# Masked copies of the second half's self probabilities on GpSimd in two operations, with new planned times

## The chip, the cores and the metric

One core of a Trainium2 chip runs the whole kernel. The core has five engines with their own instruction queues: TensorE (PE, with its weight loads as PEld), VectorE (DVE), ScalarE (ACT), GpSimd (POOL) and SyncE (SP), which only issues DMAs. The metric is the device time of one execution in microseconds, as the median of several runs.

## The reference, cut to what matters

The model is one layer: a pre-normalised attention with a recurrent memory, and an MLP. There are 2048 tokens of width 512, 32 heads of width 128, and 64 segments of 32 tokens. Each segment is attended together with 8 memory rows, and the 8 memory rows of the result are the memory of the next segment:

```python
for s in range(n_seg):                                  # 64 segments, in order
    xs = x[:, s * seg_len:(s + 1) * seg_len, :]
    h = jnp.concatenate([mem, xs], axis=1)              # 8 + 32 rows
    q, k, v = (jnp.einsum('btd,dhe->bhte', h, W) for W in (Wq, Wk, Wv))
    scores = jnp.where(mask, jnp.einsum('bhqe,bhke->bhqk', q, k) * scale, -1e9)
    o = jnp.einsum('bhqk,bhke->bhqe', softmax(scores), v)
    o = jnp.einsum('bhte,hed->btd', o, Wo)
    mem = o[:, :M, :]                                   # goes into the next segment
    outs.append(o[:, M:, :])
h = x + concatenate(outs); out = h + mlp(layernorm(h))
```

Because of `mem` the segments can't be computed side by side.

## The kernel before, in words

After a start (segment 0, which also loads the weights), the kernel runs segments 1 to 63, and then the MLP. All four segments of a 128-token block differ a little, since each carries another share of the next block's work.

In each segment, TensorE works through an order written out by hand (`ORDERS`, lines 37 to 40, one for each of the four segments of a block): the projections Q, K and V in two halves of 16 heads each, the score products of the first and the second half (SC0, SC1), units of extra projections for the next block (F0, F1), the probability products (PV0, PV1), the second softmax's product for the segment before (PVA), the output projection (WO) and the second softmax's scores (SA). The rows of a segment are dealt with in two softmaxes. The first, whose chain the change touches, covers the rows that the next segment waits for (`sc_softmax`, lines 1043 to 1065). The second (`sa_mm` and `sa_tail`, tiles SA, nma, sma, rsa, PA, PTA, BD) covers the others and is read a segment later by PVA.

For each half r (0 and 1), `sc_softmax` takes the maximum of the scores on VectorE (line 1045, `nmc`). Two exponentials on ScalarE follow, one for each of two groups sl of columns, each with its sum (line 1054, `EC` and `smc`). VectorE then makes the two reciprocals (line 1059, `rsc`) and two masked copies (line 1062, `PC`). A masked copy multiplies 64 values by the reciprocal and by a mask `even`, which is 1 or 0 by partition, and writes the result twice, once with each column of the mask. Last, VectorE transposes `PC` in blocks of 32 into `PTC` (line 1064). PV0 and PV1 (`pv_c`, line 1075) read `PTC`. The keys of these writes are PCa (sl = 0) and PC (sl = 1), with a 0 or 1 behind them for the half: PCa1 is the masked copy of sl = 0 in the second half. The reciprocals are ra and rsc, the exponentials Ea and EC.

What follows PV0 and PV1 are copies of the result to SBUF (OTm0, OTm1 for the rows that the next segment waits for, OTB for block rows, OTx0 and OTx1 for the rows of PVA), then WO, which reads them, a transpose `TT` (line 1183) and sums into `hT` (line 1177, key hTm), the next segment's memory rows.

The order on the other engines comes from a planner in the kernel (`Sched.schedule`, lines 236 to 344). TensorE's order is fixed, and everything else is taken from a heap as soon as the operations that it depends on are taken. The heap's order is a planned time: `PLAN` (lines 43 to 99) gives for each kind of operation a time from the segment's start, one for each of the four segments of a block. Once taken, an operation goes to the first gap on its engine after its inputs are ready, by estimated durations. So a planned time is a priority, and an operation planned earlier than its inputs is taken right after them. Some operations have several engines to choose from (`S.either`); the cheapest place wins, or the engine named in `HOME`.

Operations marked with `S.narrow` get a dependency on the GpSimd operation ahead of them and give one to that behind them (lines 426 to 428), so that they run strictly one after the other. The four BD copies (line 1132) and the folds of block rows (lines 1217 to 1228) are such. The folds also wait, through `tail` (line 1446), for the second half's last PC and PCa.

Of the kernel before, what the change touches and what calls it, by code (L numbers as in the profile page):

```python
# [26 lines left out]
KEEP = True  # L27
WINDOWS, WIN_LO, WIN_HI = True, 1.0, -0.8
PAUSES, PAUSE_IN, PAUSE_US = 3, 64, 0.5
HALVES = ("kq", "KA", "QT", "ZCm", "VS", "nmc", "Ea", "EC", "ra", "rsc", "PCa", "PC", "PTC", "OTm", "OTx", "KB", "QTB", "VSB")  # L30
BONUS = {}
LEAN = 0.2

# [11 lines left out]
        "ZCm0": (2.85,) * 4,  # L45
        "kq0": (2.23,) * 4,
        "KA0": (2.87,) * 4,
        "SP0": (-1.81, -1.81, -1.52, -1.65),
        "nmc0": (3.86,) * 4,
        "Ea0": (4.18,) * 4,  # L50
        "EC0": (4.59,) * 4,
        "ra0": (4.66,) * 4,
        "PCa0": (4.86,) * 4,
        "rsc0": (5.1,) * 4,
        "PC0": (5.4,) * 4,
        "PTC0": (5.74,) * 4,
        "VS0": (4.88,) * 4,
        "kq3": (2.79,) * 4,
        "QT1": (3.48,) * 4,
        "ZCm1": (3.97,) * 4,  # L60
        "kq1": (3.65,) * 4,
        "KA1": (4.29,) * 4,
        "SP1": (-1.64, -1.64, -1.36, -1.49),
        "nmc1": (5.19,) * 4,
        "Ea1": (5.51,) * 4,
        "EC1": (5.92,) * 4,
        "ra1": (5.98,) * 4,
        "PCa1": (6.1,) * 4,
        "rsc1": (6.35,) * 4,
        "PC1": (6.55,) * 4,  # L70
        "PTC1": (7.13,) * 4,
        "VS1": (6.72,) * 4,
        "OTm0": (6.56,) * 4,
        "OTm1": (7.93,) * 4,
        "OTB": (8.2, 8.48, 8.24, 8.2),
        "SAp": (7.37,) * 4,
        "nma": (10.17,) * 4,
        "SAs": (10.6,) * 4,
        "SAe": (11.07,) * 4,
        "sma": (11.54,) * 4,  # L80
        "rsa": (12.0,) * 4,
        "PA": (12.24,) * 4,
        "PTA": (13.52,) * 4,
        "BD": (15.41,) * 4,
        "OTx0": (7.22, 7.22, 7.71, 7.22),
        "OTx1": (7.71, 8.1, 8.1, 7.71),
        "TT": (9.37,) * 4,
        "hTm": (9.86,) * 4,
        "opA": (17.5, 10.96, 18.73, 17.5),
        "ZCb": (5.92, 3.35, 3.35, 3.35),  # L90
        "kq4": (10.48, 10.48, None, None),
        "KB0": (11.12, None, None, None),
        "QTB0": (None, 28.73, None, None),
        "VSB0": (None, None, 10.48, None),
        "kq5": (9.58, 8.1, None, None),
        "KB1": (12.13, None, None, None),
        "QTB1": (None, 8.75, None, None),
        "VSB1": (None, None, 7.22, None),
        "TTB": (None, None, None, 10.96)}
HOME = {('SC0', 0): 'act', 'ZCm0': 'pool', 'kq1': 'act', 'SP1': 'act', 'VS1': 'act', 'OTm0': 'act', 'SAp': 'dve', 'PA': 'pool', 'VSB1': 'act'}  # L100
STEP = 10.28
# [18 lines left out]
class Op:  # L120
# [3 lines left out]
    def __init__(self, eng, fn, reads, writes, name, dur, mode):  # L124
# [11 lines left out]
        k = writes[0] if writes else ""  # L136
        self.kind = k if isinstance(k, str) else k[0] + (str(k[-1]) if k[0] in HALVES else "")

# [418 lines left out]
ALU = mybir.AluOpType  # L557
# [53 lines left out]
def t_dve(n):  # L611
    return 0.155 + 1.0e-3 * n
# [10 lines left out]
def build_kernel(nc, A_x, A_mem0, A_Wq, A_Wk, A_Wv, A_Wo, B_w1, B_b1, B_w2, B_b2, out):  # L623
    scale = float(E) ** -0.5
    S = Sched(nc)
    st = contextlib.ExitStack()
    with st:
        def sb(name, shape, dt=BF16):
            return st.enter_context(nc.sbuf_tensor(name, shape, dt))
# [45 lines left out]
        OTB = sb("OTB", [P, 2, H, 32])  # L675
# [25 lines left out]
        def sc_place(bank):  # L701

            w = quad[:, bank, 0:128] if bank < 4 else ps[bank][:, 0:128]
            return w.rearrange("p (a n) -> p a n", a=2), ("ps", bank)
# [31 lines left out]
        for sl in range(2):  # L736
            for i in range(4):
# [20 lines left out]
             reads=["maskA"], writes=["maskA"])  # L758
# [200 lines left out]
        def v_B(bk, r, bank, back=False):  # L959
# [6 lines left out]
             reads=["ident"], writes=[("OTB", 1, sg) for sg in range(4)], dur=0.5)  # L966
# [76 lines left out]
        def sc_softmax(s, r, bank):  # L1043
            o, bkey = sc_place(bank)
            S.op("dve", lambda e: e.tensor_reduce(nmc[:, r, :], o, AX.X, ALU.max, negate=True), reads=[bkey], writes=[("nmc", r)], dur=0.28)  # L1045

            b = even[:]
            ev = bass.AP(b.tensor, b.offset, [list(b.ap[0]), [1, 2], [0, 64]])
            last = None
            for sl, names in enumerate((("Ea", "sa", "ra", "PCa"), ("EC", "smc", "rsc", "PC"))):  # L1050
                ek, sk, rk, pk = [(n, r) for n in names]

                def ex(e, sl=sl):
                    return e.activation(EC[:, r, sl, :], o[:, sl, :], ACTF.Exp, bias=nmc[:, r, sl:sl + 1], accum_out=smc[:, r, sl:sl + 1])  # L1054
                x = S.op("act", ex, reads=[("nmc", r)] + [bkey] * sl, writes=[ek, sk], dur=0.37)
                x.prev, last = last, x
            for sl, names in enumerate((("Ea", "sa", "ra", "PCa"), ("EC", "smc", "rsc", "PC"))):
                ek, sk, rk, pk = [(n, r) for n in names]
                S.op("dve", lambda e, sl=sl: e.reciprocal(rsc[:, r, sl:sl + 1], smc[:, r, sl:sl + 1]), reads=[sk], writes=[rk], dur=0.16)
                x = EC[:, r, sl, :]  # L1060
                xc = bass.AP(x.tensor, x.offset, [list(x.ap[0]), [0, 2], [1, 64]])
                S.op("dve", lambda e, sl=sl, xc=xc: e.scalar_tensor_tensor(PC[:, r, :, :, sl], xc, rsc[:, r, sl:sl + 1], ev, ALU.mult, ALU.mult),  # L1062
                     reads=[ek, rk, "even"], writes=[pk], dur=0.305)
            S.op("dve", lambda e: e.transpose(PTC[:, r].rearrange("p k t a -> p (k t a)").bitcast(F32), PC[:, r].rearrange("p k t a -> p (k t a)").bitcast(F32)),
                 reads=[("PCa", r), ("PC", r)], writes=[("PTC", r)], dur=0.31)

        def pv_c(s, r):
            par, bk, sg = s % 2, s // 4, s % 4
# [321 lines left out]
        for s in range(NS):  # L1390
# [66 lines left out]
            def part(name):  # L1457
# [18 lines left out]
                elif name in ("SC0", "SC1"):  # L1476
# [3 lines left out]
                    else:  # L1480
                        prefill("maskCF", maskCF[:].rearrange("p (a t) -> p a t", a=2), 128, o_, k_)
                    sc_mm(s, r, bank_of[name])
                    sc_softmax(s, r, bank_of[name])
                elif name in ("PV0", "PV1"):
                    pv_c(s, r)
# [65 lines left out]
            for n, lo, hi in order:  # L1551
# [4 lines left out]
                elif sg == 3 and n in ("F0", "F1"):  # L1556
                    k = 4 * (n == "F1")
# [55 lines left out]
        for k in range(NSB):  # L1613
# [13 lines left out]
            for t in range(TBS):  # L1627
                for fc in range(FC - lag, FC):
# [3 lines left out]
                     reads=[("ps", t), ("hb", bf, t)], writes=[("ob", bf, t)], after=used["WV"], dur=t_dve(512))  # L1632
# [57 lines left out]
```

## Time and profile before

| | before |
|---|---|
| median of three runs | 809.24 us (807.87 to 809.34) |
| span of the profiled execution | 805.9 us |
| instructions | 43594 |
| PE busy | 775.0 us, 96% |
| VectorE busy | 621.0 us, 77% |
| ScalarE busy | 527.1 us, 65% |
| GpSimd busy | 349.6 us, 43% |

The span goes from the first to the last instruction of the profiled execution. The page gives no other time for that execution; the runs' times hold what lies around the span too, and their median is 3.3 us longer than it. A busy share is an average over the start (to about 52 us), the body of segments 1 to 63 (to about 701 us) and the MLP (the rest). A matmul's row holds its pipelined end, so rows of successive matmuls overlap, and the distance between their starts tells more than their durations.

### The profile page before, as it was taken

How to read it: one execution, taken by the hardware profiler on the slowest of the kernel's cores; microseconds unless marked ns; L12 is line 12 of the kernel's file. 1: busy time of each engine (PE TensorE's matmuls, PEld its weight loads, DVE VectorE, ACT ScalarE, POOL GpSimd, SP SyncE). 2: the span in 40 equal slices, each digit the busy share in tenths (PEclk: the TensorE clock that was granted, in tenths of full speed). 3: DMA queues.
4: the chain of work that ended last, by engine and by line, in shares of the span. 5: the costliest groups of instructions: out<-in, count | busy, mean ns of one | idle time of the engine just before them, and what ended most of it. 6: DMA issues, size and time to landing. Idle time of an engine off the chain costs nothing.

```text
span 805.9 us, 43594 instructions
## 1 busy us (share of the span) xinstructions
PE 775.0 (96%) x19308; PEld 422.5 (52%) x18891; DVE 621.0 (77%) x2008; ACT 527.1 (65%) x1522; POOL 349.6 (43%) x886
## 2 busy tenths in 40 slices
PE   3788999999999999999999999999999999999998
PEld 1345555555555555555555555555555555544443
DVE  3268897989898989898989898989899887824211
ACT  2446777777777777777777777777676766643342
POOL 5023334545454545454545454545463535267200
PEclk9989999999999999999999999999999999999999
DMA  9950010111101010101010202020212131264200
GB/s 340 392 185 16 4 29 11 30 31 29 31 21 39 17 43 17 43 11 50 9 45 10 50 11 50 11 49 3 51 29 62 40 86 29 88 170 130 69 27 26
DMA packets 65449, 48.03 MB, mean 60 GB/s; under 512 B 29028, under 2 KB 61676, under 8 KB 65260
## 3 DMA queue, kind: packets, MB, share of 16 engines
q1 hardware_dynamic: 64928, 44.98, 19.0%
q8 instruction: 150, 2.46, 1.2%
q14 instruction: 39, 0.32, 0.1%
q10 hardware_dynamic: 332, 0.27, 0.1%
HBM read 31.08 MB, written 8.13 MB: 49 GB/s over the span
## 4 chain that ended last, share of the span: by engine, by line
PE 91%; DVE 3%; DMA 2%; SPq 2%; ACT 1%; issue 1%; POOL 0%
PE ps L872 43%; PE ps L1171 16%; PE ps L605 6%; PE quad L1579 6%; PE ps L1572 5%; PE ps L1210 4%; PE quad L1075 3%; DMA WQ<-in_A_Wq_dram 2%; SPq L775 2%; PE ps L1105 2%; PE quad L1037 2%; PE ps L1365 2%; PE quad L1143 1%; PE quad L1080 1%; DVE PC L1062 1%; ACT kq L890 1%
## 5 line engine op out<-in xcount | busy, mean ns | idle before, releaser
L872 PE MATMUL ps<-WQ,hT 128*32 128x512 bf16 x2048 | 157.4, 382 | 3.4 <-DVE hT L1177 3.3
L1171 PE MATMUL ps<-WO,OT 128*32 128x256 bf16 x4224 | 140.8, 275 | 1.0 <-ACT OT L890 1.0
L872 PE MATMUL ps<-WV,hT 128*32 128x512 bf16 x1780 | 138.7, 379 | 0.0
L891 ACT ACTIVATE kq<-ps 128x512 bf16<-128x512 f32 x146 | 87.2, 597 | 63.7 <-PE ps L872 63.4
L1126 POOL TENSOR_TENSOR PA<-SA,rsa 128x256 bf16<-128x256 f32 x64 | 39.9, 624 | 183.0 <-DVE rsa L1119 170.6
L890 ACT CAST kq<-ps 128x512 bf16<-128x512 f32 x160 | 93.4, 584 | 38.2 <-PE ps L872 38.2
L1171 PEld LDWEIGHTS ps<-WO,OT 128*32 128x32 bf16 x4224 | 96.2, 97 | 26.5 <-ACT OT L890 12.3
L1132 POOL COPY BD<-PTA 32x192 bf16<-32x192 bf16 x256 | 95.5, 373 | 16.6 <-DVE PTA L1128 0.8
L1062 DVE SCALAR_TENSOR_TENSOR PC<-EC,rsc,even 128x128 bf16<-128x128 f32 x256 | 94.5, 370 | 6.7
L872 PE MATMUL ps<-WK,hT 128*32 128x512 bf16 x1292 | 92.5, 379 | 0.0
L872 PEld LDWEIGHTS ps<-WQ,hT 128*32 128x32 bf16 x2048 | 57.0, 96 | 57.9 <-issue 18.7
L913 DVE STREAM_TRANSPOSE KALL<-kq 128x256 f32<-128x256 f32 x160 | 70.5, 440 | 20.8 <-ACT kq L890 18.6
L1054 ACT ACTIVATE EC<-quad,nmc 128x64 f32<-128x64 f32 x252 | 77.1, 311 | 5.9 <-DVE nmc L1045 0.2
L605 PE MATMUL ps<-WK,hT 128*32 128x512 bf16 x756 | 74.6, 379 | 0.0
L890 ACT CAST VS<-ps 128x512 bf16<-128x512 f32 x126 | 73.7, 585 | 0.7
L890 ACT CAST OT<-quad 128x128 bf16<-128x128 f32 (+1 forms) x205 | 66.3, 363 | 7.5 <-PE quad L1080 5.7
L913 DVE STREAM_TRANSPOSE QT<-kq 128x256 f32<-128x256 f32 x128 | 57.0, 445 | 15.5 <-ACT kq L891 14.1
L872 PEld LDWEIGHTS ps<-WV,hT 128*32 128x32 bf16 x1780 | 50.5, 96 | 34.2 <-issue 1.0
L1575 ACT ACTIVATE WQ<-ps,b1t 128x512 bf16<-128x512 f32 x42 | 28.9, 688 | 52.0 <-PE ps L1572 52.0
L872 PEld LDWEIGHTS ps<-WK,hT 128*32 128x32 bf16 x1292 | 36.4, 97 | 46.1 <-issue 20.1
L1117 ACT ACTIVATE SA<-SA 128x256 f32<-128x256 f32 x64 | 26.7, 417 | 49.4 <-DVE SA L1116 45.0
L1223 POOL TENSOR_TENSOR opT<-TTB,TTS 32x64 bf16<-32x64 f32 x128 | 40.3, 315 | 31.7 <-DVE opT L1177 22.5
(160 smaller groups left out, 1477.9 us busy)
## 6 DMA issues: line engine op xcount, KB each, us to landing
WV<-in_A_Wv_dram SPq DMA_DIRECT2D x4, 1024.0 KB, 10.3
WK<-in_A_Wk_dram SPq DMA_DIRECT2D x4, 1024.0 KB, 18.0
WQ<-in_A_Wq_dram SPq DMA_DIRECT2D x4, 1024.0 KB, 19.0
WO<-in_A_Wo_dram SPq DMA_DIRECT2D x16, 256.0 KB, 7.6
v_last<-VSB SPq DMA_DIRECT2D x60, 64.0 KB, 3.1
VBD<-v_last SPq DMA_DIRECT2D x60, 64.0 KB, 2.8
h_mid<-xr SPq DMA_DIRECT2D x16, 128.0 KB, 1.8
WQ<-h_mid SPq DMA_DIRECT2D x4, 512.0 KB, 4.4
```

What stands on the lines that cost most here:

```text
L605: return e.add_instruction(mybir.InstMatmult(name="I-%d" % (4000000 + _kept[0]), engine=mybir.EngineType.PE, start_tensor_calc=start, stop ...
L872: ins = e.matmul(o, l, m, start=(k == 0), stop=(k == DC - 1), tile_position=(0, 32 * j), skip_group_check=True)
L890: return {"act": (lambda e: e.copy(out, src), t_act(n, ps_)), "dve": (lambda e: e.tensor_copy(out, src), 0.155 + 1.0e-3 * n * fast)}
L891: return {"act": (lambda e: e.mul(out, src, scale_), t_act(n, ps_)), "dve": (lambda e: e.tensor_scalar(out, src, scale_, None, ALU.mult), ...
L913: S.op("dve", lambda e: e.transpose(out, src), reads=[("kq", i)], writes=[key], dur=t_dve(256) + 0.02)
L1054: return e.activation(EC[:, r, sl, :], o[:, sl, :], ACTF.Exp, bias=nmc[:, r, sl:sl + 1], accum_out=smc[:, r, sl:sl + 1])
L1062: S.op("dve", lambda e, sl=sl, xc=xc: e.scalar_tensor_tensor(PC[:, r, :, :, sl], xc, rsc[:, r, sl:sl + 1], ev, ALU.mult, ALU.mult), reads= ...
L1132: S.narrow(S.op("pool", lambda e, j=j, rows=rows: e.tensor_copy(BD[rows, par, :, j, :, :], PTA[rows, :, 0:NA, :]), reads=["PTA"], writes=[ ...
L1171: ins = e.matmul(ps[bank][32 * j:32 * j + 32, 0:256], lhs(slot(h)), wo_cols(h, b), start=(k == 0), stop=(k == 15), tile_position=(0, 32 * ...
L1223: return e.tensor_tensor(o[32 * q:32 * q + 32, c:c + 2], x, y, ALU.add)
L1572: ins = e.matmul(ps[bank][:, 0:SBT], W1[:, cc, fc * P:(fc + 1) * P], hnT_of(k)[:, cc, :], start=(cc == 0), stop=(cc == DC - 1))
L1579: S.op("pe", lambda e: e.matmul(quad[:, t, :], gT_of(k, fc)[:, t * P:(t + 1) * P], W2[:, fc, :], start=(fc == 0), stop=(fc == FC - 1)), re ...
```

## The change

In segments 1 to 63, for the second half only, the masked copy of sl = 0 leaves VectorE. It was one SCALAR_TENSOR_TENSOR that wrote both copies. It is now two operations on GpSimd, one for each column of the mask, both marked narrow, with the keys PCa1 and PCb1. The transpose into PTC1 waits for both. The first half, and segment 0, stay as they are.

Apart from that, some thirty rows of the planned times are changed, in many cases with another value for each of the four segments. No planned time is given to TensorE, whose order is the same. The rows that belong to the chain above, and the others that are spoken of below:

```diff
-HALVES = (..., "PCa", "PC", "PTC", ...)
+HALVES = (..., "PCa", "PCb", "PC", "PTC", ...)
...
-        "SP0": (-1.81, -1.81, -1.52, -1.65),
+        "SP0": (0.02, 1.04, 0.91, -0.12),
-        "ra0": (4.66,) * 4,
-        "PCa0": (4.86,) * 4,
+        "ra0": (4.39, 4.45, 4.45, 4.39),
+        "PCa0": (1.71, 3.51, 3.81, 3.36),
-        "PTC0": (5.74,) * 4,
+        "PTC0": (4.3, 3.88, 2.35, 3.1),
-        "ra1": (5.98,) * 4,
-        "PCa1": (6.1,) * 4,
-        "rsc1": (6.35,) * 4,
-        "PC1": (6.55,) * 4,
-        "PTC1": (7.13,) * 4,
-        "VS1": (6.72,) * 4,
-        "OTm0": (6.56,) * 4,
-        "OTm1": (7.93,) * 4,
+        "ra1": (5.38, 3.88, 5.23, 6.58),
+        "PCa1": (4.6, 4.75, 5.35, 6.1),
+        "PCb1": (5.89, 4.75, 5.89, 5.89),
+        "rsc1": (6.2, 6.35, 7.25, 4.85),
+        "PC1": (5.29, 6.49, 6.64, 6.49),
+        "PTC1": (5.72, 6.08, 4.88, 5.78),
+        "VS1": (6.03, 5.97, 5.97, 5.97),
+        "OTm0": (5.96, 5.6, 5.9, 5.9),
+        "OTm1": (7.33, 5.98, 7.18, 7.48),
-        "sma": (11.54,) * 4,
+        "sma": (7.88, 7.04, 6.98, 6.68),
-        "BD": (15.41,) * 4,
-        "OTx0": (7.22, 7.22, 7.71, 7.22),
-        "OTx1": (7.71, 8.1, 8.1, 7.71),
+        "BD": (16.07, 16.28, 15.77, 15.47),
+        "OTx0": (6.89, 7.25, 7.29, 6.8),
+        "OTx1": (9.24, 8.13, 9.33, 9.54),
-        "ZCb": (5.92, 3.35, 3.35, 3.35),
+        "ZCb": (2.71, -0.16, -0.16, 0.2),
...
                 x = EC[:, r, sl, :]
                 xc = bass.AP(x.tensor, x.offset, [list(x.ap[0]), [0, 2], [1, 64]])
+                if s > 0 and sl == 0 and r in (1,):
+                    for k in range(2):
+                        S.narrow(S.op("pool", lambda e, k=k, x=x: e.tensor_scalar(PC[:, r, k, :, 0], x, rsc[:, r, 0:1], even[:, k:k + 1], ALU.mult, ALU.mult),
+                                      reads=[ek, rk, "even"], writes=[(("PCa", "PCb")[k], r)], dur=0.25))
+                    continue
                 S.op("dve", lambda e, sl=sl, xc=xc: e.scalar_tensor_tensor(PC[:, r, :, :, sl], xc, rsc[:, r, sl:sl + 1], ev, ALU.mult, ALU.mult),
                      reads=[ek, rk, "even"], writes=[pk], dur=0.305)
             S.op("dve", lambda e: e.transpose(PTC[:, r]..., PC[:, r]...),
-                 reads=[("PCa", r), ("PC", r)], writes=[("PTC", r)], dur=0.31)
+                 reads=[("PCa", r), ("PC", r)] + [("PCb", r)] * (s > 0 and r == 1), writes=[("PTC", r)], dur=0.31)
```

More of the change, by code (lines that the diff above doesn't have):

```diff
@@ L29 @@
 PAUSES, PAUSE_IN, PAUSE_US = 3, 64, 0.5
-HALVES = ("kq", "KA", "QT", "ZCm", "VS", "nmc", "Ea", "EC", "ra", "rsc", "PCa", "PC", "PTC", "OTm", "OTx", "KB", "QTB", "VSB")
+HALVES = ("kq", "KA", "QT", "ZCm", "VS", "nmc", "Ea", "EC", "ra", "rsc", "PCa", "PCb", "PC", "PTC", "OTm", "OTx", "KB", "QTB", "VSB")
 BONUS = {}
@@ L59 @@
         "QT1": (3.48,) * 4,
-        "ZCm1": (3.97,) * 4,
+        "ZCm1": (4.3, 4.36, 4.3, 4.6),
         "kq1": (3.65,) * 4,
         "KA1": (4.29,) * 4,
-        "SP1": (-1.64, -1.64, -1.36, -1.49),
+        "SP1": (-1.58, -2.78, -1.66, -0.23),
         "nmc1": (5.19,) * 4,
@@ L66 @@
         "EC1": (5.92,) * 4,
-        "ra1": (5.98,) * 4,
-        "PCa1": (6.1,) * 4,
-        "rsc1": (6.35,) * 4,
-        "PC1": (6.55,) * 4,
-        "PTC1": (7.13,) * 4,
-        "VS1": (6.72,) * 4,
-        "OTm0": (6.56,) * 4,
-        "OTm1": (7.93,) * 4,
[L75 to L78, printed above, removed]
+        "ra1": (5.38, 3.88, 5.23, 6.58),
[7 more added lines that the diff above has]
+        "OTm1": (7.33, 5.98, 7.18, 7.48),
+        "OTB": (7.72, 9.05, 6.5, 7.6),
+        "SAp": (7.01, 7.22, 6.41, 7.37),
+        "nma": (10.11, 10.56, 10.26, 10.86),
+        "SAs": (10.15, 10.39, 10.15, 10.75),
         "SAe": (11.07,) * 4,
-        "sma": (11.54,) * 4,
-        "rsa": (12.0,) * 4,
-        "PA": (12.24,) * 4,
+        "sma": (7.88, 7.04, 6.98, 6.68),
+        "rsa": (9.6, 11.55, 10.65, 9.15),
+        "PA": (12.09, 11.49, 11.64, 10.89),
         "PTA": (13.52,) * 4,
-        "BD": (15.41,) * 4,
-        "OTx0": (7.22, 7.22, 7.71, 7.22),
-        "OTx1": (7.71, 8.1, 8.1, 7.71),
+        "BD": (16.07, 16.28, 15.77, 15.47),
+        "OTx0": (6.89, 7.25, 7.29, 6.8),
+        "OTx1": (9.24, 8.13, 9.33, 9.54),
         "TT": (9.37,) * 4,
         "hTm": (9.86,) * 4,
-        "opA": (17.5, 10.96, 18.73, 17.5),
-        "ZCb": (5.92, 3.35, 3.35, 3.35),
+        "opA": (17.23, 11.29, 19.66, 18.13),
+        "ZCb": (2.71, -0.16, -0.16, 0.2),
         "kq4": (10.48, 10.48, None, None),
@@ L94 @@
         "VSB0": (None, None, 10.48, None),
[L95 removed]
+        "kq5": (9.64, 8.16, None, None),
         "KB1": (12.13, None, None, None),
         "QTB1": (None, 8.75, None, None),
[L98 removed]
+        "VSB1": (None, None, 6.92, None),
         "TTB": (None, None, None, 10.96)}
```

## The prediction

> **What bounds the kernel now.** I read the page's busy shares first, then the busy time of two stretches of the body, and then the timeline of one segment.
>
> ```profile
> span 805.9 us, 43594 instructions
> PE 775.0 (96%) x19308; PEld 422.5 (52%) x18891; DVE 621.0 (77%) x2008; ACT 527.1 (65%) x1522; POOL 349.6 (43%) x886
> ```
> ```profile
> 92.89:586.90 494.01, 493.97 (x14020) 277.25 (x13404) 443.60 (x1472) 360.86 (x1092) 237.98 (x611) 1.00 0.11 28
> 586.90:691.30 104.40, 102.31 (x2840) 56.84 (x2822) 90.83 (x304) 74.17 (x224) 48.01 (x124) 1.00 0.18 49
> ```
> The columns of the second fence are the length, then PE, PEld, DVE, ACT and POOL busy, then the granted clock. The first row is the 48 segments 5 to 52: 494.01 / 48 = 10.29 us each, with PE never shown idle and the clock full. The second row is the ten segments 53 to 62, 10.44 us each. VectorE is busy 90% of the body, 443.60 / 48 = 9.24 us per segment, and GpSimd 48%. VectorE is the fullest helper, but what counts is where TensorE waits for it.
>
> A segment's timeline (segment 35, from 401.59 to 411.86) shows that, since a busy matmul row includes its pipelined end and so hides short waits. The rows below are TensorE's around the second half (columns: start, duration, engine, line, tiles, count).
>
> ```profile
> 402.47 0.83 PE L872 MATMUL ps<-WQ,hT 128*32 128x512 bf16 x12
> 403.11 0.61 PE L872 MATMUL ps<-WK,hT 128*32 128x512 bf16 x8
> ...
> 407.45 0.40 PE L1210 MATMUL ps<-WO,OTB 128*32 128x512 bf16 x4
> 407.79 0.27 PE L1075 MATMUL quad<-PTC,VS 64*128 64x32 bf16 x8
> ...
> 407.96 0.36 PE L1143 MATMUL quad<-BD,VS 64*128 64x48 bf16 x16
> 408.25 0.40 PE L1210 MATMUL ps<-WO,OTB 128*32 128x512 bf16 x4
> 408.55 0.62 PE L1171 MATMUL ps<-WO,OT 128*32 128x256 bf16 x16
> 409.11 0.27 PE L1075 MATMUL quad<-PTC,VS 64*128 64x32 bf16 x8
> ...
> 409.37 1.50 PE L1171 MATMUL ps<-WO,OT 128*32 128x256 bf16 x48
> 410.69 0.39 PE L1210 MATMUL ps<-WO,OTB 128*32 128x512 bf16 x4
> ```
> Twelve matmuls of 512 columns take 403.11 - 402.47 = 0.64, so a group of four is worth 0.21 us. Forty-eight of 256 columns take 410.69 - 409.37 = 1.32, so sixteen are worth 0.44. From these: the first probability product (PV0, 407.79) comes 0.34 after a group worth 0.21, WO (408.55) comes 0.30 after such a group, and the second product (PV1, 409.11) comes 0.56 after WO's sixteen, worth 0.44. A change of matmul shape takes some 0.1 of the first and the third. So PV0 may lose 0.02, WO 0.09, PV1 about nothing. These small waits are all that the body can win. The rows that end just before:
>
> ```profile
> 406.83 0.29 DVE L1045 TENSOR_REDUCE nmc<-quad 128x2 f32<-128x128 f32 x1
> 407.04 0.35 DVE L1062 SCALAR_TENSOR_TENSOR PC<-EC,rsc,even 128x128 bf16<-128x128 f32 x1
> 407.43 0.31 DVE L1064 STREAM_TRANSPOSE PTC<-PC 128x128 f32<-128x128 f32 x1
> 407.66 0.12 DVE L1059 RECIPROCAL rsc<-smc 128x1 f32<-128x1 f32 x1
> 407.82 0.37 DVE L1062 SCALAR_TENSOR_TENSOR PC<-EC,rsc,even 128x128 bf16<-128x128 f32 x1
> 408.08 0.16 DVE L1059 RECIPROCAL rsc<-smc 128x1 f32<-128x1 f32 x1
> 408.28 0.36 DVE L1062 SCALAR_TENSOR_TENSOR PC<-EC,rsc,even 128x128 bf16<-128x128 f32 x1
> 408.67 0.31 DVE L1064 STREAM_TRANSPOSE PTC<-PC 128x128 f32<-128x128 f32 x1
> ```
> ```profile
> 407.66 0.20 ACT L1054 ACTIVATION_READ_ACCUMULATOR EC<-quad,nmc 128x1 f32 x1
> 407.75 0.58 ACT L890 CAST VS<-ps 128x512 bf16<-128x512 f32 x1
> 408.21 0.67 ACT L890 CAST OT<-quad 128x128 bf16<-128x128 f32 x2
> ```
> The first half's transpose ends at 407.43 + 0.31 = 407.74 and PV0 starts at 407.79: 0.05 from one engine to the other, so PV0 does wait for VectorE. The second half's ends at 408.67 + 0.31 = 408.98; with the same 0.05 PV1 could start at 409.03, and it starts at 409.11. It has 0.08 us to spare. WO stands behind ScalarE's first OT cast, which itself follows the VS cast without a gap.
>
> **The change, part by part.**
>
> Removed: one SCALAR_TENSOR_TENSOR per segment in segments 1 to 63, the one at 407.82. It is 0.37 long, but the next instruction starts 408.08 - 407.82 = 0.26 later, so VectorE gets 63 x 0.26 = 16 us of its queue back. It belongs to the r=1 chain alone, which ends in PV1. The r=0 chain, which PV0 waits for, keeps all its instructions. The max over the second half's scores (key 5.19) still stands ahead of PC0 (5.4), so the new times don't reorder it either: PTC0 is now taken as soon as PC0 is placed, but nothing on VectorE stood between them.
>
> Added: two TENSOR_SCALAR per segment on GpSimd, each 128x64, f32 in, bf16 out. The trace has no such row. The nearest:
>
> ```profile
> L1254 POOL TENSOR_SCALAR rst<-agg 128x1 f32<-128x1 f32 x16 | 3.5, 222 | 15.9 <-DVE agg L1253 14.9
> L1223 POOL TENSOR_TENSOR opT<-TTB,TTS 32x64 bf16<-32x64 f32 x128 | 40.3, 315 | 31.7 <-DVE opT L1177 22.5
> L1225 POOL COPY TTS<-TTB 64x256 f32<-64x256 f32 x32 | 12.6, 393 | 36.2 <-DVE opT L1177 34.4 <-DVE TTB L1214 0.9
> ```
> One element takes 0.22, 64 elements of two inputs 0.315, 256 of one input 0.39. So one costs between 0.22 and 0.39; I take 0.29, near the 64-element row. Both are marked narrow, so that each waits for the one ahead of it, like the BD copies:
>
> ```profile
> 403.38 0.20 DVE L1119 RECIPROCAL rsa<-sma 128x8 f32<-128x8 f32 x1
> 403.66 0.62 POOL L1126 TENSOR_TENSOR PA<-SA,rsa 128x256 bf16<-128x256 f32 x1 [1.51 <-DVE rsa L1119]
> 405.91 1.68 POOL L1132 COPY BD<-PTA 32x192 bf16<-32x192 bf16 x4
> 407.11 0.47 POOL L1132 COPY BD<-PTA 32x192 bf16<-32x192 bf16 x1
> 408.96 0.29 POOL L829 COPY hB<-xT 128x128 bf16<-128x128 bf16 x1 [1.38 <-DMA xT<-xn]
> ```
> From VectorE to GpSimd takes 403.66 - 403.58 = 0.08. The first three BD copies take 407.11 - 405.91 = 1.20, so 0.40 each, of which about 0.06 is the step between narrow ones. GpSimd is free from 405.91 + 1.68 = 407.59 to 408.96. The queue is open, then: the first reciprocal ends at 407.78, PCa1 runs 407.86 to 408.15, PCb1 408.21 to 408.50, and with 0.08 back (taken equal to the way there; no row shows it) PTC1 could start at 408.58 instead of 408.67. Meanwhile VectorE does the second reciprocal as soon as ScalarE's accumulator has been read (407.66 + 0.20 = 407.86), then PC1 at about 408.10 to 408.47. Gain at PTC1: 0.09, and PV1 starts where it does, because it did not wait. With 0.22 each the gain is 0.23 and equally hidden. With 0.39 each PTC1 starts at 408.78, 0.11 late, of which 0.08 is slack: 0.03 lost per segment, 2 us in all.
>
> PC1 and the new pair both read EC, at the same time. The trace shows what that does: the fourth BD copy, issued at 407.11 while the SCALAR_TENSOR_TENSOR of 407.04 runs, takes 0.47, where the three before it keep a step of 0.40. So I count 0.13 us for an operation that comes second (0.47 less the 0.34 that a step of 0.40 leaves). PCb1 then ends at 408.63 and PTC1 starts at 408.71, 0.04 late and inside the slack. Were the second to wait for the whole of the first, PCb1 would start at 408.47 and end at 408.76, and PTC1 would start at 408.84: 0.17 late, 0.09 beyond the slack, 5.6 us over 62 segments. Against that stands the BD row: its 0.47 is less than the 0.28 that the other still had to run and a copy's 0.34 together. The Trainium skill (SBUF — State Buffer, "Who interferes with whom") has the harder rule: a VectorE instruction with two SBUF inputs contends with a GpSimd instruction that reads SBUF, and the later one fully blocks; by it the sum would be 5.6 us up, while the trace agrees with a wait but not with a full one.
>
> Where PV1 does wait, something can be won. In five segments without the extra projections (2, 3, 60, 61 and 62) the row of WO and that of PV1 stand further apart:
>
> ```profile
> 68.73 0.62 PE L1171 MATMUL ps<-WO,OT 128*32 128x256 bf16 x16 [0.16 <-ACT OT L890]
> 69.50 0.25 PE L1075 MATMUL quad<-PTC,VS 64*128 64x32 bf16 x7 [0.16 <-DVE PTC L1064]
> ...
> 676.55 0.27 PE L1075 MATMUL quad<-PTC,VS 64*128 64x32 bf16 x8 [0.38 <-DVE rsc L1059]
> ...
> 687.67 0.62 PE L1171 MATMUL ps<-WO,OT 128*32 128x256 bf16 x16 [0.16 <-ACT OT L890]
> 688.32 0.25 PE L1075 MATMUL quad<-PTC,VS 64*128 64x32 bf16 x7
> ```
> From WO to PV1 it is 0.77 in the first of the five and 0.65 in the last, against 0.56. The gain is 0 to 0.1 in each; I take half: 0.25 us.
>
> Moved: the planned times. They are priorities; an operation is placed in the first gap after its inputs are ready. Most moves ask for a time before its inputs (sma from 11.54 to about 7, PTC0, ZCb), which means "at once". The second softmax has room: BD ends at 407.59 and its reader starts at 407.96, even if BD's key grows by 0.6. The mask copies SP0 and the cast OTx1 go later, into the segment's idle stretches; if they collide with the hT sums at a segment's end, each 0.1 costs 6 us, but the sums' keys did not move. In every fourth segment VectorE is full up to the transpose TT:
>
> ```profile
> 441.72 0.18 DVE L807 BATCH_NORM_AGGREGATE agg<-stt 128x2 f32<-128x6 f32 x1
> 441.82 0.42 DVE L1183 STREAM_TRANSPOSE TT<-ps 128x256 f32<-128x256 f32 x1
> ```
> Here the shorter queue can pull TT forward by up to 0.04, 15 x 0.02 = 0.3 us. No DMA is added or moved past another.
>
> Sum: -0.25 - 0.3 = -0.5 us on a profiled span of 805.9. What lies around the span is 809.24 - 805.9 = 3.3 us and stays; so 808.7 for the median.
>
> **The rivals.**
>
> *The new order frees the first half (faster).* If the re-planned second softmax and casts let PC0 pass the max reduction, PV0 gets back its 0.02 in 57 segments (1.1 us), and in each of the five segments without projections, where it idles for 0.38 (the row of 676.55), the 0.21 by which the max holds PC0 up (406.83 to 407.04): 1.0 us. That is -2.1, 807.1. If WO's 0.09 went too, another 5 us: that is the low end. For it: VectorE's 16 us of room and the many keys that changed. Against it: nmc1, PC0 and rsc0 keep their keys, and ScalarE's two casts stand ahead of WO without a gap.
>
> *GpSimd's pair ends PTC1 late (slower).* It decides from the point where the pair ends after 408.67 + 0.08 - 0.08 = 408.67, that is 0.38 per operation with its waits. Price beyond that: 0.05 late is 62 x 0.05 = 3.1 us, 812.3; a full wait behind PC1 is 814.3, and of the chance below it holds 0.05. For it: two operations that read what VectorE reads. Against it: the 0.315 row has two inputs, the new ones have one.
>
> *The relief is real and not seen.* PV1's slack only grows: 809.2; it shares the forecast's case.
>
> **How the numbers follow.** This kernel's runs lie within 1.5 us, so 0.2% (1.6 us) is about what can be told from no change. Forecast and unseen relief: 0.43. First half freed, wholly or in part: 0.36. GpSimd late: 0.21. The predicted time is the forecast's, 808.7. Its own range is 807.5 to 809.8; with the others' bounds the range is 804.5 to 812.3.
>
> **What would show it.** In the profile after: SCALAR_TENSOR_TENSOR x193 instead of x256, VectorE some 16 to 23 us less busy, 126 new GpSimd rows of 0.22 to 0.39. PTC1 should start within 0.1 of 408.67 - 401.59 = 7.08 after its segment's start, and PV1 0.56 after WO. A PV1 at 0.60 or more after WO is the slow rival, a PV0 gap of 0.32 or less the fast one. A body of other than 10.2 to 10.35 us per segment makes the prediction wrong.

## The result: 2.4% slower, and the profile after

| | before | after |
|---|---|---|
| median of four runs | 808.62 us | 827.48 us (827.33 to 827.73) |
| ratio to before, with its 95% interval | | 1.0239 (1.0226 to 1.0251) |
| span of the profiled execution | 805.9 us | 825.7 us |
| one of the segments 5 to 52 | 10.29 us | 10.64 us |

The forecast was 808.7 us with a range of 804.5 to 812.3. The change cost 19 us instead. The page of after, and the same two stretches of the body (length, then PE, PEld, DVE, ACT and POOL busy, granted clock):

```profile
span 825.7 us, 43784 instructions
PE 784.0 (95%) x19308; PEld 420.0 (51%) x18891; DVE 615.1 (74%) x1961; ACT 523.6 (63%) x1506; POOL 401.8 (49%) x1012
...
L1065 POOL TENSOR_SCALAR PC<-EC,rsc,even 128x64 bf16<-128x64 f32 x126 | 52.2, 414 | 26.0 <-ACT EC L1055 19.7
```
```profile
93.94:604.42 510.48, 502.18 (x14022) 275.02 (x13407) 439.59 (x1437) 358.34 (x1080) 277.39 (x706) 1.00 0.11 27
604.42:710.98 106.56, 102.99 (x2840) 56.76 (x2822) 89.11 (x296) 73.68 (x222) 56.62 (x145) 1.00 0.18 48
```

The 48 segments take 510.48 instead of 494.01 us: 16.5 of the 19.8 us by which the span grew. The last ten give another 2.2 us. The clock is full in both, and TensorE, which before showed no idle time here (493.97 of 494.01), now shows 510.48 - 502.18 = 8.3 us of it. About half of the loss thus shows as idle time; a matmul's row, which holds its pipelined end, can hide the rest. Every kind of segment is longer (the table below). The row of line 1065 is the added work: 126 instructions as foretold, but of 0.414 us each.

The lines of VectorE (count, then busy time and mean ns, then idle time ahead of them and what ended it) show the work removed, x193 where before had x256, and a new wait:

```profile
L1070 DVE STREAM_TRANSPOSE PTC<-PC 128x128 f32<-128x128 f32 x128 | 39.9, 312 | 31.8 <-POOL PC L1065 29.6
L1068 DVE SCALAR_TENSOR_TENSOR PC<-EC,rsc,even 128x128 bf16<-128x128 f32 x193 | 70.9, 368 | 4.4
L1013 DVE COPY ps<-maskAF 128x256 f32<-128x256 f32 x31 | 12.4, 400 | 0.0
```

VectorE now stands idle for 29.6 us ahead of the transposes until GpSimd's last PC is there. The third row is one that the planner moved, the copy of maskAF: it runs on VectorE 31 times, in before twice:

```profile
L1012 DVE COPY ps<-maskAF 128x256 f32<-128x256 f32 x2 | 0.9, 428 | 0.0
```

Segment 35 of after lasts from 412.81 to 423.55. Its timeline on TensorE, then VectorE, then GpSimd (start, duration, engine, line):

```profile
412.81 0.41 PE L873 MATMUL ps<-WQ,hT 128*32 128x512 bf16 x4
...
418.67 0.40 PE L1216 MATMUL ps<-WO,OTB 128*32 128x512 bf16 x4
419.02 0.27 PE L1081 MATMUL quad<-PTC,VS 64*128 64x32 bf16 x8
...
419.77 0.62 PE L1177 MATMUL ps<-WO,OT 128*32 128x256 bf16 x16
420.52 0.27 PE L1081 MATMUL quad<-PTC,VS 64*128 64x32 bf16 x8
...
420.78 1.50 PE L1177 MATMUL ps<-WO,OT 128*32 128x256 bf16 x48
...
423.55 0.41 PE L873 MATMUL ps<-WQ,hT 128*32 128x512 bf16 x4 [0.17 <-DVE hT L1183]
```
```profile
419.31 0.37 DVE L1068 SCALAR_TENSOR_TENSOR PC<-EC,rsc,even 128x128 bf16<-128x128 f32 x1
420.15 0.31 DVE L1070 STREAM_TRANSPOSE PTC<-PC 128x128 f32<-128x128 f32 x1 [0.48 <-POOL PC L1065]
420.39 0.40 DVE L1013 COPY ps<-maskAF 128x256 f32<-128x256 f32 x1
420.82 0.52 DVE L1183 TENSOR_TENSOR opT<-TT 64x96 bf16<-64x96 f32 x2
421.35 0.56 DVE L891 CAST OT<-quad 128x384 bf16<-128x384 f32 x1
421.83 0.41 DVE L1250 TENSOR_TENSOR xr<-xr,oN 128x512 bf16<-128x512 bf16 x1
422.28 0.43 DVE L1255 BATCH_NORM_STATS2 st<-xr 128x6 f32<-128x256 bf16 x1
422.62 0.43 DVE L1189 STREAM_TRANSPOSE TT<-ps 128x256 f32<-128x256 f32 x1
```
```profile
419.11 0.94 POOL L1065 TENSOR_SCALAR PC<-EC,rsc,even 128x64 bf16<-128x64 f32 x2 [0.30 <-ACT EC L1055]
```

PV0 follows its WO group after 419.02 - 418.67 = 0.35 (before 0.34), so the first half is as it was. PV1 follows WO after 420.52 - 419.77 = 0.75 (before 0.56): 0.19 late. The rows say why: GpSimd's pair ends at 419.11 + 0.94 = 420.05, PTC1 starts at 420.15, and VectorE, done with PC1 at 419.68, waits. The other rows show a second loss: everything on VectorE behind PTC1 has moved with it. The last rows of this queue in segment 35 of before (from 401.59), behind PTC1 at 408.67, and one of ScalarE's:

```profile
408.91 0.52 DVE L890 CAST OT<-quad 128x384 bf16<-128x384 f32 x1
409.46 0.62 DVE L1177 TENSOR_TENSOR opT<-TT 64x96 bf16<-64x96 f32 x2
410.09 0.43 DVE L1244 TENSOR_TENSOR xr<-xr,oN 128x512 bf16<-128x512 bf16 x1
410.55 0.43 DVE L1249 BATCH_NORM_STATS2 st<-xr 128x6 f32<-128x256 bf16 x1
410.91 0.45 DVE L1183 STREAM_TRANSPOSE TT<-ps 128x256 f32<-128x256 f32 x1
```
```profile
408.74 0.42 ACT L1012 COPY ps<-maskAF 128x256 f32<-128x256 f32 x1
```

TT, the transpose that hT and so the next segment waits for, started 410.91 - 401.59 = 9.32 after the segment's start. In after it starts at 422.62 - 412.81 = 9.81, right behind BATCH_NORM_STATS2. That is 0.49 late, where PV1 is 0.19 late; the segment is 0.47 longer (10.74 for 10.27). PTC1 is 0.26 late here (7.34 for 7.08). The other 0.23 is a longer queue: from PTC1 to TT it is 410.91 - 408.67 = 2.24 in before and 422.62 - 420.15 = 2.47 in after. The same instructions stand between the two, the cast in another place, and ahead of them the copy of maskAF, which ScalarE did in before.

The same from the traces of all versions, over the twelve segments of each of the four kinds in a block (segments 5 to 52; kind 3 is the one shown). PV1 behind WO is a median, the length a mean, both worked out from the trace. By its medians WO starts 6.96 to 6.99 after the segment's start in every version:

```
               PV1 behind WO          segment length, by kind 0 to 3      mean
before         0.55 0.55 0.55 0.55    10.30 10.33 10.28 10.27             10.29
after          0.74 0.75 0.74 0.74    10.55 10.58 10.70 10.70             10.64
split_only     0.74 0.74 0.74 0.74    10.46 10.57 10.76 10.48             10.57
plan_only      0.55 0.55 0.55 0.57    10.30 10.33 10.27 10.43             10.33
one_on_pool    0.55 0.55 0.55 0.55    10.29 10.29 10.43 10.41             10.36
pair_const     0.55 0.55 0.55 0.55    10.30 10.32 10.44 10.50             10.39
told           0.68 0.68 0.68 0.67    10.41 10.50 10.42 10.38             10.43
told_swapped   0.75 0.75 0.75 0.74    10.49 10.57 10.52 10.45             10.51
wait_order     0.67 0.67 0.68 0.67    10.49 10.51 10.63 10.66             10.57
one_tt         0.62 0.62 0.62 0.62    10.34 10.44 10.58 10.57             10.48
one_tt_newplan 0.62 0.62 0.62 0.55    10.39 10.45 10.58 10.44             10.46
```

PV1 is equally late in all four kinds of after, but the segments are 0.25 to 0.44 longer. Where the second loss falls depends on the planned times: in split_only, which has those of before, it is largest in kind 2.

### The profile page after: what moved, and what is told of

It is laid out like the page before. It is cut to its first block, busy times and chain, and to the rows that moved or that the text cites. A ratio compares the mean times of both kernels' runs of the same rounds, so it can differ in the third digit from the quotient of the medians.

```text
span 825.7 us, 43784 instructions
## 1 busy us (share of the span) xinstructions
PE 784.0 (95%) x19308; PEld 420.0 (51%) x18891; DVE 615.1 (74%) x1961; ACT 523.6 (63%) x1506; POOL 401.8 (49%) x1012
## 5 line engine op out<-in xcount | busy, mean ns | idle before, releaser
L1177 PE MATMUL ps<-WO,OT 128*32 128x256 bf16 x4224 | 143.7, 275 | 1.7 <-ACT OT L891 1.0
L1068 DVE SCALAR_TENSOR_TENSOR PC<-EC,rsc,even 128x128 bf16<-128x128 f32 x193 | 70.9, 368 | 4.4
L891 ACT CAST OT<-quad 128x128 bf16<-128x128 f32 (+1 forms) x191 | 61.0, 350 | 19.1 <-PE quad L1086 17.6
L1065 POOL TENSOR_SCALAR PC<-EC,rsc,even 128x64 bf16<-128x64 f32 x126 | 52.2, 414 | 26.0 <-ACT EC L1055 19.7
L1070 DVE STREAM_TRANSPOSE PTC<-PC 128x128 f32<-128x128 f32 x128 | 39.9, 312 | 31.8 <-POOL PC L1065 29.6
```

The source lines that it names most:

```text
L891: return {"act": (lambda e: e.copy(out, src), t_act(n, ps_)), "dve": (lambda e: e.tensor_copy(out, src), 0.155 + 1.0e-3 * n * fast)}
L1065: S.narrow(S.op("pool", lambda e, k=k, x=x: e.tensor_scalar(PC[:, r, k, :, 0], x, rsc[:, r, 0:1], even[:, k:k + 1], ALU.mult, ALU.mult), r ...
L1177: ins = e.matmul(ps[bank][32 * j:32 * j + 32, 0:256], lhs(slot(h)), wo_cols(h, b), start=(k == 0), stop=(k == 15), tile_position=(0, 32 * ...
```

## The experiments

**The code alone (split_only).** The planned times are those of before, with PCb1 at PCa1's 6.1.

```diff
-        "PCa1": (4.6, 4.75, 5.35, 6.1),
-        "PCb1": (5.89, 4.75, 5.89, 5.89),
+        "PCa1": (6.1,) * 4,
+        "PCb1": (6.1,) * 4,
...
```

> The code part alone: the two GpSimd copies with the planned times of before (PCb1 gets PCa1's 6.1). Theory A (the pair's price): PTC1 starts 0.2 us late in every segment as in the changed kernel, PV1 follows, and the in-order VectorE queue behind PTC1 delays the rest; the planned times add nothing that can be measured: 825 to 830 us. Theory B (the planned times cost the part that PV1's own 0.19 us x 62 = 12 us leaves): 819 to 822 us.

It took 824.59 us, 1.0218 (1.0196 to 1.0239) of before: nearly the whole loss, with PV1 0.74 behind WO as in after. That is 0.4 us below the range of Theory A, and well above Theory B's.

**The planned times alone (plan_only).** The masked copy stays one SCALAR_TENSOR_TENSOR on VectorE.

```diff
-                if s > 0 and sl == 0 and r in (1,):
-                    for k in range(2): ...
-                    continue
```

> The planned times alone: VectorE keeps its SCALAR_TENSOR_TENSOR. Theory A: within 1.6 us of before, 807 to 810.5 us. Theory B: 5 to 8 us slower than before, 814 to 817 us.

809.00 us, 1.0014 (1.0000 to 1.0027): at most a small loss. In the profiled execution it lies in one kind of segment (10.43 instead of 10.27). The new times bring nothing by themselves, and the two parts add up to the whole within their intervals.

**One of the two on GpSimd (one_on_pool).** The first column of the mask stays on GpSimd, the second is a TENSOR_SCALAR on VectorE, with the planned times of before.

```diff
+                    S.narrow(S.op("pool", lambda e, x=x: e.tensor_scalar(PC[:, r, 0, :, 0], x, rsc[:, r, 0:1], even[:, 0:1], ALU.mult, ALU.mult),
+                                  reads=[ek, rk, "even"], writes=[("PCa", r)], dur=0.41))
+                    S.op("dve", lambda e, x=x: e.tensor_scalar(PC[:, r, 1, :, 0], x, rsc[:, r, 0:1], even[:, 1:2], ALU.mult, ALU.mult),
+                         reads=[ek, rk, "even"], writes=[("PCb", r)], dur=0.22)
```

> As split_only, but only the copy with the mask's first column is on GpSimd; the one with the second is a TENSOR_SCALAR on VectorE. GpSimd's single copy would end some 6.72 us into the segment, before PC1 on VectorE. Theory A: PTC1 starts within 0.1 us of where it did before and the loss is gone, 807 to 812 us. If what hurts is that VectorE and GpSimd read EC at the same time, or the hand-over itself, some 5 to 10 us of the loss stay: 814 to 820 us.

810.61 us, 1.0041 (1.0026 to 1.0056). The single operation is 0.448 us, 0.03 more than one of the pair (tile PC by line, min, median and max ns), and PV1 is on time:

```profile
L1064 POOL TENSOR_SCALAR PC<-EC,rsc,even x63: 442/448/456, 57.6 to 700.7; 128x64 bf16<-128x64 f32 x63
```

So it is the second operation in a row on GpSimd that makes PV1 late. The rest, some 3 us, lies in two kinds of segment, of which below.

**What each form costs on an idle chip (price).** Before, with four of each of nine forms on GpSimd, one after the other, on spare tiles in the MLP, where GpSimd and VectorE have little to do.

```diff
+        probe(lambda e: e.tensor_scalar(st_, xs_, r_, ev_, ALU.mult, ALU.mult))    # L1647
+        probe(lambda e: e.tensor_scalar(ct_, xs_, r_, ev_, ALU.mult, ALU.mult))    # L1648, dense output
+        probe(lambda e: e.tensor_scalar(st_, xs_, r_, None, ALU.mult))             # L1649
+        probe(lambda e: e.tensor_scalar(st_, xs_, 0.5, 1.0, ALU.mult, ALU.mult))   # L1650
+        probe(lambda e: e.tensor_scalar(st_, xs_, 0.5, None, ALU.mult))            # L1651
+        probe(lambda e: e.tensor_copy(st_, xs_))                                   # L1652
+        probe(lambda e: e.tensor_tensor(st_, xs_, xs_, ALU.mult))                  # L1653
+        probe(lambda e: e.tensor_scalar(st_[:, 0:1], xs_[:, 0:1], r_, ev_, ALU.mult, ALU.mult))   # L1654
+        probe(lambda e: e.tensor_tensor(PC[:, 1, :, :, 0], xb_, evb_, ALU.mult))   # L1655
```

> The kernel before with nine forms of a GpSimd operation, four of each, on scratch tiles in the last part of the MLP, where GpSimd and VectorE are idle; time as before. If the 0.41 us of a TENSOR_SCALAR is its own price, the same form (128x64, f32 in, bf16 out, two pointer scalars) takes 0.40 to 0.42 here too. If it is contention with VectorE's reads, it takes 0.27 to 0.32. Among the forms, the one without the second scalar, the ones with constants, the one with a dense output and the one with a single element tell which of them carries the price.

It took 808.25 us in its one run. Tile PC by line (min, median and max ns, first and last start), and the first four on the timeline:

```profile
L1647 POOL TENSOR_SCALAR PC<-EC,rsc,even x4: 412/414/416, 782.8 to 784.4; 128x64 bf16<-128x64 f32 x4
L1648 POOL TENSOR_SCALAR PC<-EC,rsc,even x4: 393/394/394, 784.9 to 786.4; 128x64 bf16<-128x64 f32 x4
L1649 POOL TENSOR_SCALAR PC<-EC,rsc x4: 457/463/481, 786.9 to 788.5; 128x64 bf16<-128x64 f32 x4
L1650 POOL TENSOR_SCALAR PC<-EC x4: 262/263/264, 789.1 to 790.1; 128x64 bf16<-128x64 f32 x4
L1651 POOL TENSOR_SCALAR PC<-EC x4: 387/388/390, 790.5 to 791.9; 128x64 bf16<-128x64 f32 x4
L1652 POOL CAST PC<-EC x4: 255/257/259, 792.3 to 793.3; 128x64 bf16<-128x64 f32 x4
L1653 POOL TENSOR_TENSOR PC<-EC x4: 295/295/296, 793.7 to 794.8; 128x64 bf16<-128x64 f32 x4
L1654 POOL TENSOR_SCALAR PC<-EC,rsc,even x4: 337/340/343, 795.2 to 796.5; 128x1 bf16<-128x1 f32 x4
L1655 POOL TENSOR_TENSOR PC<-EC,even x4: 402/402/404, 796.9 to 798.4; 128x128 bf16<-128x128 f32 x4
```
```profile
782.83 1.96 POOL L1647 TENSOR_SCALAR PC<-EC,rsc,even 128x64 bf16<-128x64 f32 x4 [25.15 <-ACT WQ L1577]
```

The form of the change costs 0.414 with nothing beside it, exactly what it costs in after: its price is its own, not contention with PC1. It is not the strided output either (0.394 dense). It is the scalars read from SBUF: two constants in their place cost 0.263, and with pointers even a single element costs 0.340. Four take 1.96 us, so the step from one narrow operation to the next is (1.96 - 4 x 0.414) / 3 = 0.10. The pair therefore needs 0.414 + 0.10 + 0.414 = 0.93 us, as after shows (0.94).

**The pair at the price I had assumed (pair_const).** After, with constants instead of the two scalars. It leaves out the reciprocal and the mask of these copies.

```diff
-e.tensor_scalar(PC[:, r, k, :, 0], x, rsc[:, r, 0:1], even[:, k:k + 1], ALU.mult, ALU.mult)
+e.tensor_scalar(PC[:, r, k, :, 0], x, 0.015625, float(1 - k), ALU.mult, ALU.mult)
```

> The changed kernel with constants in place of the two pointer scalars of the GpSimd pair; what it leaves out is the reciprocal and the mask in that group of columns. Each operation should take 0.26 us instead of 0.41. Theory A (what counts is when the pair ends): the pair ends 6.93 us into the segment instead of 7.23, PTC1 starts at about 7.04, PV1 is on time at about 7.52, and the time is 807 to 811 us. If the hand-over through GpSimd itself costs the time, or the planned times, it stays above 815 us.

812.96 us, 1.0051 (1.0031 to 1.0072), above the expected range by 2 us. PV1 is on time in every segment (0.55). The pair ends 6.97 us into the segment and PTC1 starts at 7.08 (medians), both 0.04 later than expected. The first operation of a pair takes 0.263 us, but the second takes 0.342. It starts while PC1 runs on VectorE (in the segment from 393.85 it starts at 400.49, and PC1 runs from 400.35 to 400.72). Still, that PTC1 lies within 0.1 of the 7.08 that the prediction asked for; what was lost with it is what the price of 0.414 costs, 1.0239 - 1.0051 = 1.9%, 15 us. But about 4 us remain that PV1 has no part in. They lie in kinds 2 and 3. In kind 2, ScalarE's rows and the VectorE cast ahead of them (segment from 393.85):

```profile
401.17 0.98 DVE L891 CAST OT<-quad 128x384 bf16<-128x384 f32 x2
```
```profile
401.72 0.27 ACT L1013 COPY quad<-maskCF 128x128 f32<-128x128 f32 x1 [0.16 <-DVE OT L891]
401.92 0.26 ACT L891 CAST OT<-quad 128x128 bf16<-128x128 f32 x1
```

ScalarE's last cast for WO starts 401.92 - 393.85 = 8.07 after the segment's start, where before it starts at 7.89 (median of this kind). A mask copy has been put ahead of it, and that waits for VectorE's cast. Segments of this kind are 0.16 longer. The trace of one_on_pool, which has the planned times of before, shows the same mask copy ahead of the same cast (8.05) in the same two kinds. In kind 3 of pair_const the cast is early, and it is VectorE's queue up to TT that is late (TT 9.55 instead of 9.33). So these 3 to 4 us are places that the planner chose anew once the operation had left VectorE. I read that off the traces; no run takes it away alone.

**What the planner believes (told).** After, with the pair's estimated duration at 0.5 each instead of 0.25; the same instructions, perhaps in other places.

```diff
-                                      reads=[ek, rk, "even"], writes=[(("PCa", "PCb")[k], r)], dur=0.25))
+                                      reads=[ek, rk, "even"], writes=[(("PCa", "PCb")[k], r)], dur=0.5))
```

> The changed kernel, but the planner is told 0.5 us for each GpSimd operation instead of 0.25, so that it places what follows on VectorE and ScalarE by a true time; the instructions are the same. Theory A1 (PV1's own lateness, 0.19 us x 62 = 11.6 us, stays, and the other 7 us come from a VectorE and a ScalarE queue filled in the belief that the pair is short): 818 to 822 us. Theory A2 (the other 7 us follow from the late PV1 whatever the order): 825 to 829 us.

815.65 us, 1.0091 (1.0073 to 1.0109): 12 us better than after with the same pair, and below what either theory allowed. VectorE in segment 35 (from 404.90), and GpSimd:

```profile
411.40 0.37 DVE L1068 SCALAR_TENSOR_TENSOR PC<-EC,rsc,even 128x128 bf16<-128x128 f32 x1
411.68 0.43 DVE L1013 COPY ps<-maskAF 128x256 f32<-128x256 f32 x1
412.17 0.31 DVE L1070 STREAM_TRANSPOSE PTC<-PC 128x128 f32<-128x128 f32 x1
```
```profile
411.20 0.93 POOL L1065 TENSOR_SCALAR PC<-EC,rsc,even 128x64 bf16<-128x64 f32 x2 [0.30 <-ACT EC L1055]
```

The mask copy that stood behind the wait is now ahead of it, and fills it. It is so in all segments of kinds 0 and 3, where in after the copy stood right behind PTC1. Besides, the pair ends at 411.20 + 0.93 = 412.13 and PTC1 starts 0.04 later, where in after it was 0.10. That I had not expected. The two programs differ at PTC1 in one thing: the transpose waits for two counts, VectorE's own and GpSimd's, and told lists them in the other order. The kernel itself sorts an instruction's waits by their planned end, the latest first (line 462 of after); with 0.25 per operation it plans the pair's end before PC1's, with 0.5 behind it. Two runs change that order alone.

**The order of the two waits (wait_order, told_swapped).** In wait_order, after's PTC1 waits for GpSimd first and then for VectorE's own count. In told_swapped, told's PTC1 waits in the order of after.

```diff
+                    if o.kind == "PTC1":
+                        o.waits = sorted(o.waits, key=lambda p: p.eng != "pool")     # told_swapped: != "dve"
```

> The changed kernel with the same instructions in the same order; only PTC1 waits for GpSimd's semaphore first and for VectorE's own second, instead of the other way round. In the changed kernel PTC1 starts 0.10 us after the pair's end, in the run told, which had this order, 0.035 us. If the order of the two waits makes that difference: PTC1 and PV1 0.07 us earlier in each segment, 62 x 0.07 = 4 us, 822 to 825 us. If it came from the other order of the VectorE queue in told: as the changed kernel, 826 to 829 us.

> The run told, with PTC1's two waits in the order of the changed kernel (VectorE's own first). If the order of the waits is worth 4 us: 818.5 to 821 us, and the rest of the way to the changed kernel's 827 us is what the planner's false price does to the VectorE and ScalarE queues. If it is worth nothing: 814 to 817 us.

wait_order took 823.20 us, 1.0188 (1.0169 to 1.0207); told_swapped 820.53 us, 1.0163 (1.0143 to 1.0182): both lie in the range for an order that counts. In wait_order's segment 35 the last of the pair and the transpose:

```profile
417.59 0.42 POOL L1067 TENSOR_SCALAR PC<-EC,rsc,even 128x64 bf16<-128x64 f32 x1
```
```profile
418.04 0.31 DVE L1072 STREAM_TRANSPOSE PTC<-PC 128x128 f32<-128x128 f32 x1 [0.40 <-POOL PC L1067]
```

418.04 - (417.59 + 0.42) = 0.03, against 0.10 in after. PV1 moves by the same 0.07 in both pairs of runs (0.74 to 0.67, 0.68 to 0.75). With after and told the four make a square, in ratios to before:

| | own count first | GpSimd's first |
|---|---|---|
| planner told 0.25 | 1.0239 (after) | 1.0188 |
| planner told 0.5 | 1.0163 | 1.0091 (told) |

The order of two waits is worth 0.0051 and 0.0072, which is 4 to 6 us of 809 (62 x 0.07 = 4.3). The planner's wrong price, with the order of the waits the same, is worth 0.0076 and 0.0097, 6 to 8 us. Since that price also set the order, all of 1.0239 - 1.0091 = 1.5%, 12 us, comes from it. What remains in told is 0.0091 or 7.4 us, as much as PV1's remaining lateness of 0.12 would cost: 62 x 0.12 = 7.4.

**One GpSimd operation without pointers (one_tt, one_tt_newplan).** VectorE multiplies the mask by the reciprocal (128x2), and one TENSOR_TENSOR of 128x128 on GpSimd writes both copies; in one_tt with the planned times of before, in one_tt_newplan with the new ones.

```diff
+                    S.op("dve", lambda e: e.tensor_scalar(re[:], even[:], rsc[:, r, 0:1], None, ALU.mult), reads=[rk, "even"], writes=[("PCb", r)], dur=0.13)
+                    S.op("pool", lambda e, xc=xc, re_=re_: e.tensor_tensor(PC[:, r, :, :, 0], xc, re_, ALU.mult),
+                         reads=[ek, ("PCb", r)], writes=[("PCa", r)], dur=0.45)
```

> The planned times of before, and one GpSimd operation in place of the pair: VectorE multiplies the two mask columns by the reciprocal (128x2), and GpSimd multiplies EC by that in one TENSOR_TENSOR of 128x128, 0.40 us in the idle part of the MLP. The result is the whole computation. It should end about 6.85 us into the segment and PTC1 start at about 6.98, 0.1 earlier than before. Theory A: 806 to 809 us, at most 0.5 us of gain, since PV1 did not wait before. If any hand-over through GpSimd costs time: 811 us or more.

> As one_tt, with the new planned times. Theory A: as the planned times alone, 807 to 811 us. If the new times are worth something once the GpSimd part ends early, 803 to 806 us.

one_tt took 819.34 us, 1.0131 (1.0115 to 1.0148), one_tt_newplan 817.09 us, 1.0108 (1.0092 to 1.0125). one_tt is 10 us above its Theory A, and one_tt_newplan lies above both of its ranges. GpSimd and VectorE in one of its segments (from 407.84), then the same in one_tt_newplan (from 406.88):

```profile
414.38 0.40 POOL L1067 TENSOR_TENSOR PC<-EC,re 128x128 bf16<-128x128 f32 x1 [0.54 <-DVE rsc L1061]
```
```profile
414.40 0.55 DVE L1070 SCALAR_TENSOR_TENSOR PC<-EC,rsc,even 128x128 bf16<-128x128 f32 x1
415.05 0.31 DVE L1072 STREAM_TRANSPOSE PTC<-PC 128x128 f32<-128x128 f32 x1
```
```profile
413.55 0.44 POOL L1067 TENSOR_TENSOR PC<-EC,re 128x128 bf16<-128x128 f32 x1 [0.67 <-DVE re L1066]
```
```profile
413.37 0.37 DVE L1070 SCALAR_TENSOR_TENSOR PC<-EC,rsc,even 128x128 bf16<-128x128 f32 x1
414.02 0.31 DVE L1072 STREAM_TRANSPOSE PTC<-PC 128x128 f32<-128x128 f32 x1 [0.27 <-POOL PC L1067]
```

The GpSimd operation costs its 0.40 and ends at 414.78, in time. But VectorE's PC1, issued 0.02 behind it, takes 0.55 instead of 0.37 and ends at 414.95; it sets PTC1. PTC1 then starts 0.10 behind PC1's end, where in before, with a single wait, it is 0.03 (so also the medians over segments 5 to 52). Here GpSimd's count is listed first and VectorE's own, the one that comes last, second: the price of the second place again, though the engine is another. Of the 0.12 by which PTC1 is late (7.21 for 7.10), 0.04 is PC1's later end and 0.07 this. Where the order is the other way round, in the second version, PC1 takes 0.37, the GpSimd operation 0.44, and PV1 in that kind of segment is on time (0.55). So here two engines do stand in each other's way, and the one issued first wins. The Trainium skill (SBUF — State Buffer, "Who interferes with whom") states that order of issue decides, for a VectorE instruction with two SBUF inputs beside a GpSimd instruction that reads SBUF; these rows agree with that. They don't agree with a full block, which that section states for a VectorE instruction in a 2-port mode and the prediction counted for this one: PC1 issued at 414.40 and held until 414.78 would end at about 415.15, and it ends at 414.95. Nor is the rule seen in after, where PC1 starts inside the first TENSOR_SCALAR of the pair (419.31, with it running to 419.52) and takes 0.37 as ever.

At 62 x 0.07, PV1's lateness would make 4.3 of one_tt's 10.6 us. The rest lies mainly in kinds 2 and 3, 0.30 longer each. There the same mask copy as in pair_const stands ahead of ScalarE's last cast for WO, which starts at 8.20 instead of 7.89. No run takes that away alone.

No version that was run beats before.

## Why the prediction was wrong

**The mechanism was a rival in it, and its size was wrong.** "GpSimd's pair ends PTC1 late" had a chance of 0.21, with the point of decision at 0.38 per operation and a price of 3.1 us. It is what happened, at six times that price.

The step that failed first is "so one costs between 0.22 and 0.39; I take 0.29". The upper bound was itself below the truth of 0.414. I bounded by the number of elements, and all three rows lacked what sets this price: the scalars read from SBUF. The trace of before held a sign that the number of elements is no bound: a GpSimd TENSOR_TENSOR of one element (line 809, `rst<-rst,cneg`, a power) takes 0.57. The row of 0.222 is a TENSOR_SCALAR of one element without a pointer; with two pointers one element costs 0.340. I had bounded from both sides, but with rows that all lay on one side in this respect, and I did not open the bound for it.

The smaller terms of the same sum: the step between narrow operations was 0.10 and not 0.06, the hand-over from GpSimd to VectorE 0.10 and not 0.08, and the contention of 0.13 did not occur: the second operation takes 0.417, the first 0.412 (medians). The longer first operation had pushed the second nearly past PC1 (419.62, with PC1 done at 419.68). In pair_const, where it starts earlier, the second takes 0.08 more than the first, so the term was not empty. In all the pair with its hand-over took 0.94 + 0.10 = 1.04 where the sum had 408.71 - 407.86 = 0.85 with contention. PTC1 came 7.33 after the segment's start (before 7.10), 0.24 late; PV1 came 0.19 late, so 0.05 of the slack that I put at 0.08 was there.

**Lateness times 62 gives 12 of the 19 us.** The rival's price counted PV1 alone. That fits where the planner knows the price: told loses 7.4 us with PV1 0.12 late, and told_swapped 13 with PV1 0.19 to 0.20 late. But by it after would lose 62 x 0.19 = 12 us, and it lost 19. I had asked what is queued behind SCALAR_TENSOR_TENSOR and not what is queued behind PTC1, which now waits at the head of VectorE's queue for 0.48 us (29.6 us over the kernel). A planner that believes 0.25 per operation puts copies behind the wait instead of ahead of it, and they hold up TT. With the waits in the same order and PV1 equally late, told_swapped is 6 us faster than after.

**Planned times.** The 0.3 us from a shorter queue in every fourth segment did not come: even in pair_const TT of that kind (2) starts later, 9.49 instead of 9.37. Alone, the new times cost at most 0.3%. "VectorE some 16 to 23 us less busy" failed also: it was 621.0 - 615.1 = 5.9 us. The planner filled the room with copies and casts from ScalarE (the maskAF copies grew from 0.9 to 12.4 us). The gain of 0.25 us in the segments without projections is too small to be told from anything here.

**What held:** x193 and x126 as counted, the first half and WO where they were (WO at 6.96 to 6.99 in all versions), the sign of the slow rival (PV1 at 0.60 or more behind WO), and that VectorE's relief is worth nothing while TensorE sets the pace: even with the pair on time, pair_const is not faster.

## What to carry to other kernels

Work that leaves a busy engine for an idle one must be priced by the very form of the instruction, the kind of its scalars included; where the trace has no row with the same operands, the upper bound must stay open, or a few forms are timed on an idle stretch first. A late input costs more than its lateness times the count, if the waiting instruction stands at the head of a queue with due work behind it: the planner's estimate for a moved operation must be right before its places are. And an engine that is 90% busy isn't a bound so long as another engine's end sets the step.

## What the runs showed of the hardware

- GpSimd's TENSOR_SCALAR, 128x64 f32 to bf16: 0.263 us with two constants, 0.414 with two pointers, and 0.463 with one pointer alone and 0.388 with one constant alone. That one scalar costs more than two is not explained by any run.
- An instruction with two waits, the later of which is GpSimd's, started 0.10 us after GpSimd's end with its own engine's count listed first, and 0.03 with GpSimd's listed first. In two pairs of runs that moved PV1 by 0.07. In one_tt, where VectorE's own count comes last and is listed second, it was 0.10 too; in one_on_pool, where it comes last and is listed first, 0.03. Why is open.
- The GpSimd TENSOR_TENSOR of 128x128 lengthened VectorE's SCALAR_TENSOR_TENSOR from 0.37 to 0.55 when issued first, and was itself lengthened from 0.40 to 0.44 when issued second. Two-pointer TENSOR_SCALARs did not lengthen it at all (0.37). A two-constant TENSOR_SCALAR that started inside it took 0.34 instead of 0.26. What makes that difference wasn't tried.
